# Retention in chunks of 64 tokens, two per visit, every product a 64x64 quarter of the array

## The chip, the cores and the metric

The kernel runs on one core of a Trainium2 chip. The metric is device time in microseconds (us), the median of several executions; for the kernel before it is 926.88 us over three runs (925.43 to 928.27). All times below that belong to an instruction come from one profiled execution.

## The reference: what is computed

Three layers follow one another on a batch of 8 sequences of 576 tokens. First comes retention with 8 heads of 64 channels, a causal product of queries, keys and values in which every pair of tokens is weighted with a power of the head's decay:

```
scores = q @ k.T / 8                       # per batch and head, 576 x 576
ret    = scores * gamma[h] ** (i - j)      # only where i >= j, else 0
x      = ret @ v                           # heads side by side: 576 x 512
```

Then a mixture of four single-head attentions (projections of x to 64 channels for q, k and v, causal softmax, output projection, the two best experts of four by a gate). Last a token and channel mixer (`x @ w_theta`, cosine and sine of it, two 576x576 token products, one 512x512 channel product).

Retention is not computed as 576 x 576 scores. The tokens are cut into chunks. Inside a chunk the masked scores are multiplied with the values; what lies before the chunk enters through a state, a 64x64 matrix per head, the running sum of `k.T @ v`, that is multiplied with the queries. The decays are put into the values and into a factor on the result, so that the mask is only 0 and 1.

## The kernel before

The first half of the program (to about 436 us) is one loop over 80 units: batch, expert pair, row block of attention (five row blocks of 128, 128, 128, 128 and 64 tokens). TensorE's order is the order in which the program is written (a manual schedule); the other engines' orders are laid down by a scheduler before the run. Ten units, numbered 0 to 9 here as *slots*, make one batch, and into the slots of batch b the retention of batch b+1 is woven. `SLOTS` says what each slot holds besides its attention: projections (`Q01`, `K10`, `v0` ...) and visits of the retention `R0` to `R5`. In this document an attention row block shows on TensorE as scores (`w<-KK,U`, line 309), transposes of the probabilities (`w<-ident,P`, line 356) and, in groups of row blocks, the outputs (`w<-PT,V`, line 375, function `at_out`), whose operand PT is copied out of the transposes' PSUM by VectorE (DVE) and ScalarE (ACT), line 361.

A visit Rc works on chunks of 128 tokens in four steps:

- `ret_values(c-1)`: the state's update (line 154, 128 rows by 64 columns of the array, two products side by side), the state's copy to SBUF by ACT (line 156), and scores times values (line 161, same half-width form)
- the attention outputs that are due
- `ret_state(c-1)`: state times queries (line 173, quarters of 64x64, 128 columns of data), then DVE multiplies the result with the decays into xt (line 181), ACT and GpSimd split xt into high and low parts
- `ret_scores(c)`: scores of the next chunk (line 132, quarters of 64x64, 128 or 64 columns), masked by DVE in six instructions per chunk (line 138 four times on 64 partitions, line 141 twice on 128)

All of these are fp32 products; each one shows as two records in the trace. The PSUM has eight banks: seven tiles `w` in a ring (`WB = 7`), through which all scores, transposes, projections, outputs and retention results go in the order of the program, and one bank `pS` for the state. A tile of the ring can be written again when the engine that reads it is done with the tile that had that place before, seven tiles earlier.

The chunks of batch 0 are done ahead of the loop, in the prologue. The last batch has a list of its own (`LAST`), with tiles of the mixer's first steps in place of retention; the second half of the program (480 us to the end) is the mixer.

Of the kernel before, what the change touches and what calls it, by code (L numbers as in the profile page):

```python
# [21 lines left out]
C = 128  # L22
# [5 lines left out]
NCONST = 256 + 192 + NCH * H + 1088 + E * E + 4 * (128 + NCH)  # L28
# [14 lines left out]
SLOTS = [("Q01 K10", "R0"), ("", ""), ("K11 Q10", ""), ("Q11", "R1"), ("", "R2"),  # L43
# [3 lines left out]
WB = 7  # L47
# [12 lines left out]
def tile_kernel(ctx: ExitStack, tc: tile.TileContext, qk, kv, w1, wo, wot, wd, cst, out):  # L60
# [21 lines left out]
    tri = att.tile([128, 3, 64], F32, name="tri")  # L82
    gam = att.tile([128, NCH, H], F32, name="gam")
# [8 lines left out]
    SB = [ret.tile([128, 4, D], F32, name=f"S{i}") for i in range(2)]  # L92

    SMT = [[ret.tile([128, 2, 2, 128], F32, name=f"sm{i}{q}") for q in range(2)] for i in range(2)]
# [14 lines left out]
    def loads(b, c):  # L109
        R = ROWS[c]  # L110
        o = c * 1024
        t = ret.tile([128, 8, R], F32, name="kt", bufs=LDB, padded_shape=[128, 8, 128])
        nc.sync.dma_start(t, qk[b, :, o:o + 8 * R].rearrange("p (h r) -> p h r", h=8))
        u = ret.tile([128, 2, DM], F32, name="kv", bufs=LDB)
        nc.sync.dma_start(u, kv[b, c * C:c * C + C, :].rearrange("r (a d) -> r a d", a=2))
        vp = ret.tile([128, H, D], F32, name="vp", bufs=VPB)
        MARK["pool"] = nc.gpsimd.tensor_mul(vp, u[:, 1, :].rearrange("p (h d) -> p h d", h=H),
                                            gam[:, c, :, None].to_broadcast([128, H, D]))
        QKT[b, c], KVT[b, c], VP[b, c] = t, u, vp

    def ret_scores(b, c):

        R = ROWS[c]
        t = QKT[b, c]
        ps = [ps1.tile([128, 2, 2, 128], F32, name="w", bufs=WB) for _ in range(2)]
        for i in range(2):
            for e, j in ((0, 0), (1, 0), (1, 1), (0, 1)):
                if j * 64 < R:
                    g = slice((e ^ j) * 64, (e ^ j) * 64 + 64)
                    for s in range(2):  # L130
                        r = slice(s * 64, s * 64 + 64)
                        nc.tensor.matmul(ps[s][g, i, e, j * 64:R], t[r, 4 + 2 * i + e, j * 64:j * 64 + 64],  # L132
                                         t[r, 2 * i + e, j * 64:R], start=True, stop=True, skip_group_check=True)
        sm = SMT[(b * NCH + c) % 2]
        for s in range(2):
            for e in range(2):
                g = slice(e * 64, e * 64 + 64)
                nc.vector.tensor_mul(sm[s][g, :, e, :64], ps[s][g, :, e, :64],  # L138
                                     tri[g, 2, None, :].to_broadcast([64, 2, 64]))
            if R > 64:  # L140
                nc.vector.tensor_mul(sm[s][:, :, :, 64:], ps[s][:, :, :, 64:],  # L141
                                     tri[:, None, 0:2, :].to_broadcast([128, 2, 2, 64]))
        SM[b, c] = sm

    def ret_values(b, c):
        R = ROWS[c]
        t, u, vp, sm = QKT.pop((b, c)), KVT.pop((b, c)), VP.pop((b, c)), SM.pop((b, c))
        if c == 0:
            PSS[b] = ps1.tile([128, 4, D], F32, name="pS", bufs=1, padded_shape=[128, 4, 128])
        if c < NCH - 1:  # L150
            pS = PSS[b]
            for h in range(H):
                s = h % 2 * 64
                nc.tensor.matmul(pS[s:s + 64, h // 2, :], u[:, 0, h * D:h * D + D], vp[:, h, :],
                                 start=c == 0 and h < 2, stop=False, skip_group_check=True)
            nc.scalar.activation(SB[(c + 1) % 2], pS, AF.Copy)
        px = [ps1.tile([128, 2, R], F32, name="w", bufs=WB, padded_shape=[128, 2, 256]) for _ in range(2)]
        for s in range(2):
            for i in range(2):
                for e in range(2):  # L160
                    nc.tensor.matmul(px[s][e * 64:e * 64 + 64, i, :], vp[:, 4 * i + 2 * e + s, :], sm[s][:, i, e, :R],
                                     start=i == 0, stop=not c and i == 1, skip_group_check=True)
        PX[b, c] = t, px

    def ret_state(b, c):
        R = ROWS[c]
        t, px = PX.pop((b, c))
        Sb = SB[c % 2]
        for i in range(2 if c else 0):
            for e in range(2):  # L170
                for s in range(2):
                    r, hp = slice(s * 64, s * 64 + 64), 2 * i + e
                    nc.tensor.matmul(px[s][e * 64:e * 64 + 64, i, :], Sb[r, hp, :], t[r, hp, :],
                                     start=False, stop=i == 1, skip_group_check=True)
# [5 lines left out]
        for s in range(2):  # L180
            nc.vector.tensor_mul(xt[:, 2 * s:2 * s + 2, :], px[s], gt[:, 2 * s:2 * s + 2, cs])
# [7 lines left out]
    def ret_out(b, c):  # L189
        ret_values(b, c)  # L190
        ret_state(b, c)

    def ret_first(b, names):
        for n in names.split():
            if n[0] == "R" and n != "R0" and b + 1 < B:
                ret_values(b + 1, int(n[1]) - 1)

    def ret_second(b, names):
        for n in names.split():
            if n[0] == "R" and b + 1 < B:  # L200
                c = int(n[1])
                if c:
                    ret_state(b + 1, c - 1)
                if c < NCH:
                    ret_scores(b + 1, c)
# [29 lines left out]
    def proj_v(b, c):  # L235
# [14 lines left out]
        nc.scalar.copy(V[:R, c, :, :], pv)  # L250
# [114 lines left out]
    def at_out(b, p, g):  # L365
# [13 lines left out]
        nc.scalar.copy(OB[b, p][:, ms[0] * C:ms[0] * C + W], po)  # L379
# [12 lines left out]
    o = 448  # L392
    nc.sync.dma_start(gam, cst[:, o:o + NCH * H].rearrange("p (c h) -> p c h", c=NCH))
    for s in range(2):
        for sm in SMT:
            for e in range(2):
                nc.gpsimd.memset(sm[s][64 - 64 * e:128 - 64 * e, :, e, :64], 0.0)
# [5 lines left out]
    nc.sync.dma_start(tri, cst[:, 256:448].rearrange("p (a q) -> p a q", a=3))  # L403
# [96 lines left out]
    ret_scores(0, 0)  # L500
    make_gt(0)
    ret_scores(0, 1)
    ret_out(0, 0)
    make_gt(1)
    for kt in range(4):
        split_w1(kt)
        if kt == 1:
            ret_out(0, 1)
# [3 lines left out]
    work(-1, "v0 v1")  # L512
    for c in range(2, NCH):
        ret_scores(0, c)
        ret_out(0, c)
        work(-1, ("", "v2 k00", "q00 v3 k01 v4 g")[c - 2])
# [13 lines left out]
    def token_tile(pp, g, i):  # L530
# [14 lines left out]
        if pp is ps1:  # L545
            if i % 2:
                th = pp.tile([128, DM], F32, name="w", bufs=WB)
            else:
                th = pp.tile([128, 4, 128], F32, name="pS", bufs=1).rearrange("p a d -> p (a d)")
# [51 lines left out]
    for t in range(nu + 1):  # L601
# [11 lines left out]
        if t == nu - 1:  # L613
# [3 lines left out]
            zp = pool("zp")  # L617
        if t:
# [4 lines left out]
        if b < B - 1:  # L623
            ret_first(b, between)
        else:
            work(b, between)
        if between or b == B - 1:
# [3 lines left out]
        if b < B - 1:  # L631
            ret_second(b, between)
# [249 lines left out]
```

## Time and profile before

| | |
|---|---|
| median of 3 runs | 926.88 us (925.43 to 928.27) |
| the profiled execution | 925.94 us, of which 924.2 us are the span of its instructions |
| TensorE (PE) matmuls busy | 887.6 us, 96% |
| VectorE (DVE) | 661.9 us, 72% |
| ScalarE (ACT) | 440.4 us, 48% |
| GpSimd (POOL) | 223.8 us, 24% |
| mean granted TensorE clock | 0.991 |

The busy time of PE is the time in which at least one matmul was under way, and matmuls overlap, so a busy PE may still stand behind a wait. What a run of matmuls costs is therefore read from the start of its first record to the start of the run that follows.

### The profile page before, as it was taken

To read this page: it belongs to the slowest core of one execution; us is meant where nothing else is said; L and a number is where in the kernel's file an instruction comes from. 1 tells how busy PE (TensorE), PEld (TensorE's weight loads), DVE (VectorE), ACT (ScalarE), POOL (GpSimd) and SP (SyncE) were. 2 spreads that over 40 slices of the span, in tenths; PEclk is the share of its full clock that TensorE was granted. 3 is DMA by queue.
4 is the path that set the end of the run, shared out by engine and by line. 5 is a ranking of instruction groups with operands and counts; after the bars stand their busy time and mean duration, and the time that the engine had idled before them with its cause. 6 is when DMAs were issued, how large, how long until landed. Compare 5 with 4: busy or idle time off the path is not lost.

```text
span 924.2 us, 22725 instructions
## 1 busy us (share of the span) xinstructions
PE 887.6 (96%) x8526; PEld 817.3 (88%) x8526; DVE 661.9 (72%) x2003; ACT 440.4 (48%) x1166; POOL 223.8 (24%) x276
## 2 busy tenths in 40 slices
PE   7899989999999999999999899999999999999998
PEld 6788978888888888888878899999999999999998
DVE  6487776877879787787777976766668674777632
ACT  2265645556556555555666533434334432444320
POOL 4316153361534525243121102102020110101010
PEclk8999999999999999999999899999999999999999
DMA  8667665776666776655685442343513333151311
GB/s 308 198 165 211 174 182 159 199 211 177 197 185 176 230 192 198 166 163 141 192 276 192 126 93 65 70 115 87 145 33 76 90 79 90 27 135 24 92 34 52
DMA packets 146205, 132.27 MB, mean 143 GB/s; under 512 B 83376, under 2 KB 121648, under 8 KB 146096
## 3 DMA queue, kind: packets, MB, share of 16 engines
q1 hardware_dynamic: 145952, 130.55, 50.5%
q8 instruction: 67, 1.10, 0.5%
q0 software_dynamic: 144, 0.28, 0.2%
q14 instruction: 42, 0.34, 0.1%
HBM read 80.20 MB, written 32.00 MB: 121 GB/s over the span
## 4 chain that ended last, share of the span: by engine, by line
PE 55%; DVE 7%; DMA 4%; ACT 3%; issue 2%; SPq 1%; POOL 1%; ACTq 0%; DVEq 0%; POOLq 0%
PE acc L712 22%; PE w L97 8%; PE w L99 8%; PE w L98 8%; PE w L375 3%; PE w L247 2%; PE w L309 2%; DMA KK<-KN 1%; ACT P L317 1%; DVE sm L138 1%; PE w L356 1%; DMA wost<-wot 1%; DMA og<-gd 1%; PE w L132 1%; DVE cs L577 1%
## 5 line engine op out<-in xcount | busy, mean ns | idle before, releaser
L712 PE MATMUL acc<-TK,zh 128*128 128x256 f32 (+1 forms) x1024 | 181.4, 300 | 3.9 <-DVE u L726 3.2
L712 PEld LDWEIGHTS acc<-TK,zh 128*128 128x128 f32 x1024 | 156.2, 192 | 4.5 <-ACT cs L575 3.4
L317 ACT ACTIVATE P<-P,st 128x128 f32<-128x128 f32 (+4 forms) x160 | 95.7, 600 | 68.0 <-DVE st L312 67.6
L712 PE MATMUL acc<-TK,zl 128*128 128x256 f32 (+1 forms) x512 | 110.7, 298 | 0.0
L728 POOL TENSOR_TENSOR ul<-u,uh 128x576 fp32r<-128x576 f32 x16 | 24.3, 1541 | 324.2 <-ACT uh L727 237.0
L712 PEld LDWEIGHTS acc<-TK,zl 128*128 128x128 f32 x512 | 87.4, 192 | 0.0
L102 ACT ACTIVATE zh<-cs 128x512 fp32r<-128x512 f32 x64 | 40.3, 631 | 90.1 <-PE acc L712 70.6
L375 PE MATMUL w<-PT,V 128*64 128x192 f32 (+3 forms) x576 | 67.1, 329 | 14.5 <-DVE PT L361 8.1
L97 PE MATMUL w<-xh,WH 128*128 128x288 f32 x256 | 76.6, 299 | 2.9 <-DVE sm L141 2.6
L103 DVE TENSOR_TENSOR zl<-cs,zh 128x512 fp32r<-128x512 f32 x64 | 44.9, 706 | 48.0 <-ACT zh L102 46.4
L309 PE MATMUL w<-KK,U 128*64 128x288 f32 (+4 forms) x384 | 77.8, 329 | 0.9 <-DMA KK<-KN 0.9
L575 ACT ACTIVATE cs<-cs 128x512 f32<-128x512 f32 x72 | 45.1, 631 | 67.4 <-DVE cs L573 54.0
L98 PE MATMUL w<-ul,CH 128*128 128x256 f32 (+1 forms) x256 | 75.7, 296 | 0.0
L375 PEld LDWEIGHTS w<-PT,V 128*64 128x64 f32 (+1 forms) x576 | 43.0, 138 | 36.9 <-ACT PT L361 13.2
L99 PE MATMUL w<-uh,CH 128*128 128x256 f32 (+1 forms) x256 | 75.7, 296 | 0.0
L97 PE MATMUL w<-uh,CH 128*128 128x256 f32 (+1 forms) x256 | 75.5, 297 | 0.1
L98 PE MATMUL w<-xl,WH 128*128 128x288 f32 x256 | 75.3, 294 | 0.0
L99 PE MATMUL w<-xh,WL 128*128 128x288 f32 x256 | 75.3, 294 | 0.0
L312 DVE CUSTOM_DVE_ANT_0 P<-w,cm 128x128 f32<-128x128 f32 (+4 forms) x160 | 72.2, 476 | 1.8 <-PE w L309 1.3
L138 DVE TENSOR_TENSOR sm<-w,tri 64x128 f32<-64x128 f32 x160 | 45.4, 284 | 25.5 <-PE w L132 17.7
L451 POOL TENSOR_TENSOR r<-r,ex 128x192 f32<-128x192 f32 (+1 forms) x51 | 29.5, 578 | 140.3 <-ACT P L317 52.0
L577 DVE SCALAR_TENSOR_TENSOR cs<-cs,x 128x512 f32<-128x512 f32 x72 | 48.8, 688 | 18.8 <-ACT cs L575 18.3
(142 smaller groups left out, 2192.5 us busy)
## 6 DMA issues: line engine op xcount, KB each, us to landing
kv<-kv SPq DMA_DIRECT2D x40, 512.0 KB
KK<-KN SPq DMA_DIRECT2D x128, 144.0 KB
kt<-qk SPq DMA_DIRECT2D x32, 512.0 KB
raw<-wd SPq DMA_DIRECT2D x43, 192.0 KB
xd<-xb SPq DMA_DIRECT2D x126, 64.0 KB
out<-u SPq DMA_DIRECT2D x28, 288.0 KB
u<-xd SPq DMA_DIRECT2D x28, 288.0 KB
td<-hl SPq DMA_DIRECT2D x27, 192.0 KB
```

Source lines behind the costliest of these rows:

```text
L97: nc.tensor.matmul(ps, ah, bh, start=first, stop=False)
L98: nc.tensor.matmul(ps, ah, bl, start=False, stop=False)
L99: nc.tensor.matmul(ps, al, bh, start=False, stop=last)
L103: nc.vector.tensor_sub(l, src, h)
L138: nc.vector.tensor_mul(sm[s][g, :, e, :64], ps[s][g, :, e, :64], tri[g, 2, None, :].to_broadcast([64, 2, 64]))
L309: nc.tensor.matmul(ps[s][:R], U[:, s, rs], KK[:, s, x, j0:j1], start=x == 0, stop=x == 1)
L312: MARK["dve"] = nc.vector.tensor_tensor_reduce(Ps[s][:R, j0:j1], ps[s][:R], cm[:R, o + j0:o + j1], 1.0, st[:R, 0, s:s + 1] if i else 3.0e3 ...
L317: MARK["act"] = nc.scalar.activation(Ps[s][:R, :n], Ps[s][:R, :n], AF.Exp, bias=st[:R, last, s:s + 1], scale=-1.0, accum_out=SUM[p][:R, m, ...
L375: nc.tensor.matmul(po[s * 64:s * 64 + 64, c0:], V[:ROWS[j], j, 2 * p + s, :], v, start=j == 0, stop=j == last, skip_group_check=True)
L575: nc.scalar.activation(cs, cs, AF.Sin)
L577: nc.vector.scalar_tensor_tensor(z, cs, -1.0, x2[:, None, ds].to_broadcast([128, 2, 256]), op0=OP.mult, op1=OP.mult)
L712: nc.tensor.matmul(acc[d][j], A[:, dc], TK[:, kt, W, t0:t1], start=q == 0 and n == 0, stop=q == 8 and n == 2)
```

## The change

Retention works on chunks of 64 tokens. A visit still handles two of them (128 tokens), but every product, scores, values, state and queries, is now 64 rows by 64 columns of the array with 64 columns of data, written in an order that goes round the four quarters. The operands are laid out on the host so that the halves of the partitions hold different heads.

The state of the first chunk of a visit is updated at the end of the visit before (`ret_state(2c)`), that of the second inside the visit (`ret_state(2c+1)`); four copies `S` in SBUF take turns. Products on different row halves of the array write to different PSUM banks, so the state has two banks and the ring is left with six (`WB = 6`). State times queries must write both banks from both row halves; it is cut into two parts, `ret_query(..., 0)` and `ret_query(..., 1)`, in which the row halves change banks, and the first product of the second part gets an explicit wait on an instruction of another engine that comes after the first part: the copy of the state by ACT, or in R5 the mask by DVE.

One attention output is issued inside each visit, between the next chunk's scores and the second query part. Outputs come later by one visit in part: that of slot 0 runs in slot 1 (`"O"`) before that slot's transposes, and of the two that fell into slot 3 one moves to slot 4. R0, the first scores of a batch, moves from slot 0 into R5 of the batch before. The mask is two DVE instructions per visit. State copies by ACT are eight per batch instead of four.

```diff
-SLOTS = [("Q01 K10", "R0"), ("", ""), ("K11 Q10", ""), ("Q11", "R1"), ("", "R2"),
+SLOTS = [("Q01 K10", ""), ("", "O"), ("K11 Q10", ""), ("Q11", "R1"), ("", "R2"),
          ("v0", "R3"), ("v1", ""), ("v2 k00", "R4"), ("q00", "R5"), ("v3 k01 v4 g", "")]
-WB = 7
+WB = 6
...
     def ret_scores(b, c):
+        for j in range(n):
+            for i in range(2):
+                for v in range(2):
                     for s in range(2):
+                        x = 2 * v + i
+                        nc.tensor.matmul(ps[s][half(v), j, i, :], t[half(s), 4 + x, half(j)], t[half(s), x, half(j)],
+                                         start=True, stop=True, skip_group_check=True)
...
+            MARK["sync"] = nc.vector.tensor_mul(sm[s][:, :n], ps[s][:, :n], tri[:, None, None, :].to_broadcast([128, n, 2, 64]))
...
+    def ret_state(b, k):
+        c, j = divmod(k, 2)
...
+            PSS[b] = ps1.tile([128, 2, 512], F32, name="pS", bufs=1)
...
+        MARK["sync"] = nc.scalar.activation(SB[(k + 1) % 4], pS[:, :, :2 * D].rearrange("p v (i d) -> p v i d", i=2), AF.Copy)
...
+    def ret_query(b, c, cross, sync=None):
...
+                for s in range(2):
+                    v = s ^ cross
+                    mm = nc.tensor.matmul(px[v][half(i), s, j, :], SB[k % 4][half(s), v, i, :],
+                                          t[half(s), 2 * v + i, half(j)], start=False, stop=False, skip_group_check=True)
+                    if sync:
+                        tc.add_manual_dep(mm.ins, sync.ins.name, SYNC, reason="the row halves change banks")
+                        sync = None
...
+    def ret_step(b, c, nx, other):
+        if c >= 0:
+            ret_values(b, c)
+            ret_query(b, c, 0)
+            MARK["sync"] = None
+            if c < NCH - 1:
+                ret_state(b, 2 * c + 1)
+            done = MARK["sync"]
+        if nx:
+            ret_scores(*nx)
+        other()
+        if c >= 0:
+            ret_query(b, c, 1, done or MARK["sync"] or MARK["out"])
+            ret_end(b, c)
+        if nx and nx[1] < NCH - 1:
+            ret_state(nx[0], 2 * nx[1])
...
+    ret_step(0, 2, (0, 3), lambda: work(-1, "v0"))
+    ret_step(0, 3, (0, 4), lambda: work(-1, "v1"))
+    ret_step(0, 4, None, lambda: work(-1, "v2 k00"))
+    ret_step(1, -1, (1, 0), lambda: None)
+    work(-1, "q00 v3 k01 v4 g")
...
+        if between == "O":
+            for o in outs:
+                at_out(*o)
+            outs = []
         if t:
             at_trans(units[t - 1])
...
+            if between[:1] == "R":
+                def other():
+                    at_out(*outs.pop(0))
+                c = int(between[1])
+                x = b + 1
+                ret_step(x, c - 1, (x, c) if c < NCH else (x + 1, 0) if x + 1 < B else None, other)
```

On TensorE, slot 4 of a batch (visit R2) before, from the last transposes to the next unit's scores; the shapes are partitions by columns of the result:

```order
L356 MATMUL w<-ident,P 128x128 x8
L154 MATMUL pS<-vp,kv 64x64 x8
L161 MATMUL w<-sm_135,vp 64x128 x4
L161 MATMUL w<-sm_136,vp 64x128 x4
L173 MATMUL w<-kt,S_134 64x128 x8
L132 MATMUL w<-kt 64x128 x4
L132 MATMUL w<-kt 64x64 x4
L132 MATMUL w<-kt 64x128 x4
L132 MATMUL w<-kt 64x64 x4
L309 MATMUL w<-KK,U 128x128 x4
```

The same slot now, from the second half of the values on (line 166 is line 161 of before, 179 is 173, 153 is 154, 135 is 132, 391 is 375, 325 is 309):

```order
L166 MATMUL w<-sm_137,vp 64x64 x4
L166 MATMUL w<-sm_138,vp 64x64 x4
L179 MATMUL w<-kt,S_135 64x64 x4
L179 MATMUL w<-kt,S_136 64x64 x4
L153 MATMUL pS<-vp,kv 64x64 x8
L135 MATMUL w<-kt 64x64 x16
L391 MATMUL w<-PT,V 64x256 x4
L391 MATMUL w<-PT,V 64x128 x2
L179 MATMUL w<-kt,S_135 64x64 x4
L179 MATMUL w<-kt,S_136 64x64 x4
L153 MATMUL pS<-vp,kv 64x64 x8
L325 MATMUL w<-KK,U 128x128 x4
```

An attention output of half-width form (line 391) has come in between scores and the second query part, and the state stands twice, once ahead of the scores and once at the end.

On ACT, the same slot before, from the output of slot 3 to the split of xt (S is the state's copy, P the exponentials of the unit's row block, PT the copy that the attention outputs read, r and hl weight conversions):

```order
L379 COPY ob<-w 128x256
L156 ACTIVATE S_133<-pS 128x256
L317 ACTIVATE P,sum_126<-P,st 64x576 x2
L361 COPY PT<-w 128x4x128
L450 ACTIVATE r<-raw 128x192
L183 ACTIVATE xh<-xt 128x4x128
```

And now (line 333 is 317, 377 is 361, 462 is 450, 464 is 452, 155 is 156, 395 is 379, 199 is 183):

```order
L333 ACTIVATE P,sum_126<-P,st 64x576 x2
L377 COPY PT<-w 128x4x128
L462 ACTIVATE r<-raw 128x192
L464 ACTIVATE hl<-b_4439 128x192
L155 ACTIVATE S_133<-pS 128x256
L395 COPY ob<-w 128x256
L155 ACTIVATE S_134<-pS 128x256
L199 ACTIVATE xh<-xt 128x4x128
```

The state's copy, which stood ahead of the two exponentials, has moved behind them, behind the PT copy and behind two conversions; the second query part on TensorE waits for the first of the two copies.

## Rows read from the trace of the kernel before

**Rows 1.** Windows: us, busy PE, PEld, DVE, ACT, POOL; granted clock, DMA share, GB/s

```profile
0.00:44.38 44.38, 35.08 (x498) 30.75 (x499) 24.61 (x52) 12.13 (x26) 18.08 (x32) 0.92 0.80 259
212.32:268.47 56.15, 54.31 (x692) 48.32 (x690) 45.07 (x169) 33.25 (x106) 23.16 (x31) 1.00 0.68 193
```

**Rows 2.** Lines by form, PE, retention: line, rows*columns of array, form, records | busy, mean

```profile
L161 PE MATMUL w<-sm,vp 128*64 128x128 f32 x512 | 34.2, 274 | 2.4 <-DVE sm L141 2.4
L132 PE MATMUL w<-kt 64*64 64x128 f32 x512 | 25.4, 277 | 1.4 <-DMA kt<-qk 1.4
L132 PE MATMUL w<-kt 64*64 64x64 f32 x640 | 23.8, 217 | 0.0
L154 PE MATMUL pS<-vp,kv 128*64 128x64 f32 x512 | 21.9, 228 | 0.0
L173 PE MATMUL w<-kt,S 64*64 64x128 f32 x384 | 16.6, 280 | 0.0
L161 PE MATMUL w<-sm,vp 128*64 128x64 f32 x128 | 6.2, 230 | 0.8 <-DVE sm L138 0.8
L173 PE MATMUL w<-kt,S 64*64 64x64 f32 x128 | 3.7, 230 | 0.0
```

**Rows 3.** Timeline, PE, visit R2 (slot 4): start us, us, line, form, records

```profile
235.28 0.69 PE L154 MATMUL pS<-vp,kv 128*64 128x64 f32 x16
235.79 1.05 PE L161 MATMUL w<-sm,vp 128*64 128x128 f32 x16
236.77 0.67 PE L173 MATMUL w<-kt,S 64*64 64x128 f32 x16
237.26 0.85 PE L132 MATMUL w<-kt 64*64 64x128 f32 x32
238.03 0.44 PE L309 MATMUL w<-KK,U 128*128 128x128 f32 x2
```

**Rows 4.** Timeline, PE, visit R5 (slot 8), last chunk of 64 tokens

```profile
258.66 0.69 PE L161 MATMUL w<-sm,vp 128*64 128x64 f32 x16
259.18 0.61 PE L375 MATMUL w<-PT,V 128*64 128x256 f32 x2
260.51 1.30 PE L375 MATMUL w<-PT,V 128*64 128x256 f32 x10 [0.73 <-ACT PT L361]
261.74 0.46 PE L173 MATMUL w<-kt,S 64*64 64x64 f32 x16
262.13 0.61 PE L309 MATMUL w<-KK,U 128*64 128x288 f32 x3
```

**Rows 5.** Waits to 440 us: who waited for whom: us in total, times, longest

```profile
PEld w L173 <- issue: 4.1, 24, 0.2
PE w L375 <- DVE PT L361: 7.3, 12, 3.0
PE w L375 <- ACT PT L361: 5.7, 11, 0.7
```

**Rows 6.** Lines by form to 440 us, masks on DVE, state copies on ACT

```profile
L138 DVE TENSOR_TENSOR sm<-w,tri 64x128 f32<-64x128 f32 x160 | 45.4, 284 | 25.5 <-PE w L132 17.7 <-DMA tri<-cst 6.4
L141 DVE TENSOR_TENSOR sm<-w,tri 128x256 f32<-128x256 f32 x64 | 27.2, 425 | 0.9
L156 ACT ACTIVATE S<-pS 128x256 f32<-128x256 f32 x32 | 12.4, 387 | 28.2 <-PE pS L154 28.2
```

**Rows 7.** Timelines of slots 3 and 4: transposes (PE), U and xt (DVE), PT (ACT)

```profile
228.21 0.82 PE L356 MATMUL w<-ident,P 128*128 128x128 f32 x6
...
230.34 0.93 DVE L233 SCALAR_TENSOR_TENSOR U<-w,U 64x288 fp32r<-64x288 f32 x2
...
238.10 0.56 ACT L361 COPY PT<-w 128x512 f32<-128x512 f32 x1
```

**Rows 8.** Timeline, PE, prologue, chunk 2 of batch 0

```profile
24.43 0.69 PE L154 MATMUL pS<-vp,kv 128*64 128x64 f32 x16
25.77 0.66 PE L161 MATMUL w<-sm,vp 128*64 128x128 f32 x8 [0.65 <-DVE sm L141]
```

More of the change, by code (lines that the diff above doesn't have):

```diff
@@ L113, in loads @@
         nc.sync.dma_start(t, qk[b, :, o:o + 8 * R].rearrange("p (h r) -> p h r", h=8))
[L114 to L118, printed above, removed]
+        n = R // 64
@@ L121, in ret_scores @@
     def ret_scores(b, c):
-        R = ROWS[c]
+        n = ROWS[c] // 64
         t = QKT[b, c]
[L125 to L129, printed above, removed]
+        ps = [ps1.tile([128, 2, 2, 64], F32, name="w", bufs=WB, padded_shape=[128, 4, 2, 64]) for _ in range(2)]
+        for j in range(n):
+            for i in range(2):
+                for v in range(2):
@@ L143, in ret_scores @@
-        SM[b, c] = sm
-    def ret_values(b, c):
-        R = ROWS[c]
[L147 to L163, printed above, removed]
@@ new lines, in ret_scores @@
+        SM[b, c] = sm
+    def ret_state(b, k):
+        c, j = divmod(k, 2)
+        u, vp = KVT[b, c], VP[b, c]
+        if k == 0:
+            PSS[b] = ps1.tile([128, 2, 512], F32, name="pS", bufs=1)
+        pS = PSS[b]
+        for i in range(2):
+            for s in range(2):
+                for v in range(2):
+                    x = 2 * s + i
+                    nc.tensor.matmul(pS[half(s), v, i * D:i * D + D], u[half(v), j, 0, x * D:x * D + D], vp[half(v), j, x, :],
+                                     start=k == 0 and i == 0, stop=False, skip_group_check=True)
+        MARK["sync"] = nc.scalar.activation(SB[(k + 1) % 4], pS[:, :, :2 * D].rearrange("p v (i d) -> p v i d", i=2), AF.Copy)
@@ new lines, in ret_values @@
+    def ret_values(b, c):
+        n = ROWS[c] // 64
+        vp, sm = VP[b, c], SM.pop((b, c))
+        px = [ps1.tile([128, 2, 2, 64], F32, name="w", bufs=WB, padded_shape=[128, 4, 2, 64]) for _ in range(2)]
+        PX[b, c] = px
+        for j in range(n):
+            for s in range(2):
+                for i in range(2):
+                    for v in range(2):
+                        nc.tensor.matmul(px[v][half(i), s, j, :], vp[half(v), j, 2 * s + i, :], sm[s][half(v), j, i, :],
+                                         start=j == 0 and s == 0, stop=False, skip_group_check=True)
@@ L175, in ret_state, with ret_end @@
+    def ret_end(b, c):
+        R = ROWS[c]
+        px = PX.pop((b, c))
+        for x in (QKT, KVT, VP):
+            x.pop((b, c))
         cs = slice(c * C, c * C + R)
@@ L249, in proj_v @@
         pv = ps[:R, :E * D].rearrange("p (e d) -> p e d", e=E)
-        nc.scalar.copy(V[:R, c, :, :], pv)
+        MARK["out"] = nc.scalar.copy(V[:R, c, :, :], pv)
         nc.scalar.activation(l[:R, c, :], ps[:R, E * D:], AF.Copy)
@@ L391, in tile_kernel @@
         nc.tensor.matmul(pw, warm, warm, start=True, stop=True)
[L392 to L397, printed above, removed]
+    o = 320
+    nc.sync.dma_start(gam, cst[:, o:o + NCH * H].rearrange("p (c j h) -> p c j h", c=NCH, j=2))
     for l in LG:
```

115 lines of the change are left out of this document (41 added, 74 removed).

## Prediction

> **What bounds the kernel now.** I read the windows of the profile first: busy time of each engine, batch by batch. In a typical batch TensorE (PE) is busy for 54.3 of 56.2 us, DVE for 45.1, ACT for 33.3 [rows 1]; the loop over the 80 units is bound by PE, with DVE second. Seven batches carry visits, and the prologue (44.4 us, PE busy 35.1) carries the retention of batch 0 [rows 1]. The second half of the program does not change.
>
> The groups by line and form come next: how many records of each kind retention has [rows 2]. Their mean durations are no price, since matmuls overlap. The price is read from the timeline of one visit, from the start of a run to the start of the next [rows 3, 4]. Then the waits [rows 5]: where PE stands, it stands before an attention output, for the copy PT. All runs are at the same clock level, so the prices carry over.
>
> **Prices from rows.**
> - State, half-width, 64 columns: 16 records from 235.28 to 235.79, 32 ns each [rows 3].
> - Values, half-width, 128 columns: 16 from 235.79 to 236.77; about 0.1 us of it belongs to the change of form that follows, so 55 ns each [rows 3]. With 64 columns (16 from 258.66 to 259.18) 32 ns [rows 4].
> - Quarters, 128 columns: 16 from 236.77 to 237.26, less 0.05 us for the change ahead: 27.5 ns [rows 3].
> - Quarters, 64 columns: 16 from 261.74 to 262.13, 0.39 us, of which one whole change of form (0.17, below) is taken off: 14 ns [rows 4]. The mixed run of 32 scores confirms it: 16 x 27.5 + 16 x 14 = 0.66, and 0.77 is seen with the change behind it [rows 3].
> - A change of the array's form: PE idles 4.1 us in 24 cases ahead of line 173, with nothing waited for that the profile shows: 0.17 us each [rows 5].
>
> **The change part by part.**
>
> *Products.* Before: 512 x 55 + 128 x 32 (values), 512 x 32 (state), 384 x 27.5 + 128 x 14 (queries), 512 x 27.5 + 640 x 14 ns (scores): 28.2 + 4.1 + 16.4 + 10.6 + 1.8 + 14.1 + 9.0 = 84.2 us, counts from [rows 2]. Now a batch has nine chunks of 64: 72 products for scores, 72 for values, 64 for state, 64 for queries, 272 in all, two records each; in eight batches 4352 records of the 64-column quarter kind, at 14 ns 60.9 us. The sum falls by 23.3 us. The number of records rises by half, so this term hangs on the 14 ns. They are seen in runs of 16 records; the new runs are about 100 long. From the other side the price is bounded by the 27.5 ns of the wider quarters: then the term is 119.7 - 84.2 = 35.5 us of loss. I take the 14 ns, because those rows have exactly the new form.
>
> *Changes of form.* Before, each of six visits goes full, half, quarter, full: 18 per batch. Now the five visits that are left go full, quarter, half (the output), quarter, full, and slot 1's output alone makes two: 22. Four more in seven batches at 0.17 us cost 4.8 us. The Trainium skill, "TensorEngine Tiling (Array Packing)", section Key Properties, says that changing the tiling mode drains TensorE. The trace agrees with 0.17 us a time, and this is the one rule that speaks against writing an output into the middle of a visit; it costs a fifth of what the products give.
>
> *Waits that go.* PE idles 13.0 us in 23 cases before outputs for PT [rows 5]. The idle time counts from the modelled end of the record before; in R5 the start stands 1.33 us behind a pair of records that fills 0.22, so 1.1 us are lost where 0.73 are noted [rows 4]. With 0.35 more each, the waits are 13.0 + 23 x 0.35 = 21 us, 3 per batch. In the new order the outputs in slots 1, 3 and 4 belong to an earlier slot, and their PT has long been copied; the others have a visit's products ahead of them as before. I take all 21 out and count what remains as new waits.
>
> *New waits.* Four places, per batch.
>  - Slot 3: the ring of six. The second tile of the next scores takes the bank that the projection `Q11` had. DVE is done with that at 230.34 + 0.93 = 231.27, 2.3 us after the transposes' run ended at 228.96 (start of the state's run there) [rows 7]. PE reaches the scores after a change 0.17, values 0.45, queries 0.11, state 0.22: 0.95. It waits 1.3. With seven banks and two outputs ahead of the scores it did not.
>  - Slot 4: the second query part waits for the state's copy, which on ACT has moved behind two exponentials, PT and two conversions. PT ends at 238.66 [rows 7], then three instructions of about 0.39, the copy's own mean [rows 6] (an estimate for the other two): 239.83, 4.55 us after the transposes' run (235.28). PE needs it after 0.17 + 0.45 + 0.22 + 0.22 + 0.45 + 0.17 and an output of about 1.3 + 0.17 (ten records took 1.23 with their change [rows 4]): 3.15. That would be 1.4 of wait. But the exponentials hang on DVE, and a visit's masks fall from 4 x 0.284 + 2 x 0.425 = 1.99 to 0.85 us [rows 6]: 1.14 earlier. I take 0.5, between 0.3 and 1.4. Queued behind the waiting product on PE are the rest of the visit and the next scores; DVE's xt and with it two banks of the ring wait for them.
>  - Slot 5: the first tiles after that visit take the banks of its two results, free only when xt is done, which DVE does after masks and conversions: 1.0, between 0.4 and 2.0.
>  - Slot 8: the output still waits for PT; products ahead of it take 1.1 instead of 0.5 us: 0.5 left of 1.1.
>  Together 3.3 per batch, 23 us in seven; from 1.3 (only slot 3) to 6.0 per batch, 9 to 42 us.
>
> *DVE and ACT.* Masks are 64 x 0.425 + 16 x 0.284 = 31.7 us instead of 72.6 [rows 6]: 41 us less on the second engine. ACT gains 32 copies at 0.387, 12.4 us [rows 6], beside 12 us per batch in which it has nothing to do at PE's pace. Neither is added: the loop goes by PE, and what they move is in the waits above.
>
> *Prologue.* The values of chunks 2 to 4 stand between state and mask, as at 24.43 + 0.51 to 25.77, 0.83 us [rows 8], and again ahead of their second half. Now scores run a visit ahead, with projections in between; but two of these start later, and R0 is added. I take 3 us, between 6 gained and 1 lost, beyond the prologue's share of the products. The last batch goes on with six banks where seven were; nothing to 2 us, not in the sum.
>
> **Sum:** -23.3 + 4.8 - 21 + 23 - 3 = -19.5 us. The profiled execution took 925.94, close to the median of 926.88; off the median that is 907 us.
>
> **Rivals.**
> 1. *The waits eat it.* The ring of six and the copy's place cost the upper end, 6.0 per batch (42 instead of 23), and the last batch's 2: 907 + 19 + 2 = 928. For it: DVE and ACT work in a fixed order and lag by 2 to 4.5 us in slots 3 to 5 [rows 7]. Against it: the masks' 1.14 us per visit fall in just these slots.
> 2. *The other side: long runs of quarters don't keep 14 ns.* Place: the block of about 100 records in each visit. Price: at 21 ns, midway to the wider quarters' rate, 4352 x 7 ns = 30 us, so 938; at 27.5 ns 59 us, so 966. It decides from 14 + 19.5 / 4.352 = 18.5 ns. For it: PE must be handed a record and its weights every 14 ns for 1.4 us on end; before, only short stretches ask for that, and the 48 records from 236.77 to 238.03 average 26 ns [rows 3]. Against: in that same stretch the 64-column records behind the wide ones still fit 14. The Trainium skill, "TensorE: Matmul & The Clock Gate", section Wait - 56ns, not 53.3ns?, says that the distance from start to start never falls below about 25 ns, however few the columns; by that the products would cost 109 us instead of 61. The rows disagree where four quarters take turns: 0.39 us for 16, even with the change counted in, is 24 ns, and 14 without.
> 3. *DVE's relief pays more.* If shorter masks let PT, the state's copy and the banks come in time everywhere but slot 3, the new waits are 9 us: 907 - 14 = 893.
>
> **How the numbers follow.** The forecast 907 has 0.60, its own range 896 to 920; the waits (928) 0.16, the slow quarters (938 and above) 0.11, the relief (893) 0.13. The range of 889 to 928 leaves out most of the slow quarters, half of the first rival's upper side and the far end of the third. Within 0.3% is 924.1 to 929.7, about what three runs of this kernel can tell from no change. Faster than that: 0.58 of the forecast's 0.60, 0.05 of the first rival, all of the third: 0.76. Within: 0.02 + 0.06 = 0.08. Slower: 0.11 + 0.05 = 0.16.
>
> **What the profile after will show.** 64-column quarter records at 14 ns from start to start in a visit, about 1.4 us from values to scores without a wait (right), or 20 and more (rival 2). PE waits of lines 391 and 179 and of the ring in slots 3 to 5: about 3 us a batch (right), 6 (rival 1), 1 (rival 3). A batch of 56 us should take about 54, the prologue about 39. DVE's busy time should fall by 41 us and ACT's rise by 12 in the first half. The forecast is wrong if a batch still takes 56, or if the waits at outputs have not moved.

## The result, and the profile after

The changed kernel takes **910.2 us** (median of 4 runs, 910.16 to 912.79) against 926.8 us (925.43 to 928.27) beside it: ratio 0.982, 95% interval 0.980 to 0.984, so 16.6 us faster by the medians. The forecast was 907. The profiled execution of the changed kernel took 912.79 us, the longest of the four, so the two traces show 13.2 of the 16.6 us.

From the start of one slot's attention scores to the next, the trace says where: the prologue takes 41.0 us instead of 44.4, the seven batches with visits 382.2 instead of 391.9, the rest of the program the same (484.1 and 484.6, to the end of the last matmul). But by the same measure a batch of the changed kernel holds more waits than was thought. The windows of prologue and one batch after (columns as in [rows 1]):

```profile
0.00:41.02 41.02, 31.94 (x738) 29.52 (x739) 17.67 (x36) 13.90 (x31) 16.01 (x24) 0.88 0.82 273
207.25:262.08 54.83, 51.56 (x884) 46.30 (x882) 45.63 (x151) 34.86 (x110) 22.98 (x31) 1.00 0.67 193
```

A batch is 1.3 us shorter than the one in [rows 1], and PE is busy for 2.7 us less of it: half of what PE no longer does has become idle time. DVE is no less busy in this batch than in the one before, although its masks are lighter (the last section says what took their place).

The lines by form after, retention on PE, masks and state copies (to be held against [rows 2] and [rows 6]):

```profile
L179 PE MATMUL w<-kt,S 64*64 64x64 f32 x1024 | 32.8, 229 | 6.5 <-ACT S L155 5.6 <-ACT ob L395 0.5
L135 PE MATMUL w<-kt 64*64 64x64 f32 x1152 | 29.0, 226 | 6.3 <-ACT lg L267 2.6 <-DVE PT L379 2.0 <-DMA kt<-qk 1.3
L153 PE MATMUL pS<-vp,kv 64*64 64x64 f32 x1024 | 27.5, 222 | 3.7 <-POOL vp L118 3.7
L166 PE MATMUL w<-sm,vp 64*64 64x64 f32 x1152 | 26.8, 229 | 3.0 <-DVE sm L139 3.0
...
L139 DVE TENSOR_TENSOR sm<-w,tri 128x256 f32<-128x256 f32 x64 | 23.8, 413 | 14.1 <-PE w L135 8.1 <-DMA tri<-cst 5.7
L139 DVE TENSOR_TENSOR sm<-w,tri 128x128 f32<-128x128 f32 x16 | 3.9, 285 | 6.5 <-PE w L135 6.5
...
L155 ACT ACTIVATE S<-pS 128x256 f32<-128x256 f32 x64 | 24.4, 382 | 25.9 <-PE pS L153 25.9
```

The 4352 records are there, idle time stands before all four groups, masks cost 27.7 us instead of 72.6, state copies 24.4 instead of 12.4. Visit R2 of the changed kernel, the counterpart of [rows 3], with ACT's side of it below:

```profile
226.85 0.70 PE L166 MATMUL w<-sm,vp 64*64 64x64 f32 x32
227.37 0.41 PE L179 MATMUL w<-kt,S 64*64 64x64 f32 x16
227.60 0.41 PE L153 MATMUL pS<-vp,kv 64*64 64x64 f32 x16
227.83 0.65 PE L135 MATMUL w<-kt 64*64 64x64 f32 x32
228.41 1.30 PE L391 MATMUL w<-PT,V 128*64 128x256 f32 x12
230.64 0.46 PE L179 MATMUL w<-kt,S 64*64 64x64 f32 x16 [0.93 <-ACT S L155]
230.92 0.41 PE L153 MATMUL pS<-vp,kv 64*64 64x64 f32 x16
231.26 0.91 PE L325 MATMUL w<-KK,U 128*128 128x128 f32 x3
```

```profile
228.50 0.56 ACT L377 COPY PT<-w 128x512 f32<-128x512 f32 x1
228.97 0.38 ACT L462 ACTIVATE r<-raw 128x192 f32<-128x192 uint32 x1
229.95 0.36 ACT L464 ACTIVATE hl<-b 128x192 fp32r<-128x192 f32 x1 [0.60 <-DVE b L459]
230.22 0.36 ACT L155 ACTIVATE S<-pS 128x256 f32<-128x256 f32 x1
```

From 226.85 to 227.83 stand 64 quarter records in 0.98 us, 15 ns each with one step of 87 ns behind the fourth, where 39 are usual, counted in. Then the second query part waits for the state's copy, which stands on ACT behind PT and two conversions, the second of which waits for DVE itself. In slot 8 (R5), which answers to [rows 4], the wait has changed sides, from the output to the ring:

```profile
251.65 0.28 PE L135 MATMUL w<-kt 64*64 64x64 f32 x2
252.43 0.69 PE L135 MATMUL w<-kt 64*64 64x64 f32 x30 [0.51 <-DVE PT L379]
253.05 1.30 PE L391 MATMUL w<-PT,V 128*64 128x256 f32 x12
```

The waits of PE from 40 to 430 us, after ([rows 5] has those of before; L377 and L379 are the copies PT, L263 the projection of the values, L98 the others):

```profile
PE w L179 <- ACT S L155: 5.6, 10, 1.6
PE w L263 <- POOL xl L200: 4.2, 2, 2.7
PE w L135 <- ACT lg L267: 2.6, 5, 0.7
PE w L98 <- POOL xl L200: 2.5, 5, 1.0
PE w L391 <- ACT PT L379: 2.4, 7, 0.4
PE w L325 <- DVE sm L139: 2.2, 4, 1.0
PE w L135 <- DVE PT L379: 2.0, 4, 0.5
```

The view's rows sum to 15.6 us before and 23.1 after. The outputs hardly wait any more (13.0 to 2.7), and much around them does.

The two waits of line 263 for xl, the longest of all (2.7 us), have another cause than the copies. Both times xl stands on GpSimd right behind `vp<-kv,gam` (line 118, the values of a later chunk times the decays), and GpSimd sits idle until the load of kv is there, a DMA transfer: 7.11 us until 73.57 and 2.77 us until 130.65. xl starts 1.0 and 1.2 us after vp.

### The profile page after: what moved, and what is told of

Its sections match the earlier page's. It is cut to its first block, busy times and chain, and to the rows that moved or that the text cites. A ratio compares the mean times of both kernels' runs of the same rounds, so it can differ in the third digit from the quotient of the medians.

```text
span 910.9 us, 25606 instructions
## 1 busy us (share of the span) xinstructions
PE 866.0 (95%) x10062; PEld 800.9 (88%) x10062; DVE 645.3 (71%) x1859; ACT 454.4 (50%) x1198; POOL 220.2 (24%) x268
## 4 chain that ended last, share of the span: by engine, by line
PE 66%; DVE 14%; DMA 8%; ACT 5%; issue 3%; POOL 2%; SPq 1%; ACTq 0%; POOLq 0%; DVEq 0%
PE acc L730 22%; PE w L98 9%; PE w L97 9%; PE w L99 9%; PE w L263 4%; PE w L325 3%; DMA kv<-kv 3%; PE w L391 3%; PE w L372 2%; ACT P L333 2%; DVE P L328 2%; DMA KK<-KN 2%; DVE U L249 1%; DVE xt L196 1%; DVE sm L139 1%
## 5 line engine op out<-in xcount | busy, mean ns | idle before, releaser
L103 DVE TENSOR_TENSOR zl<-cs,zh 128x512 fp32r<-128x512 f32 x64 | 47.5, 745 | 48.0 <-ACT zh L102 47.5
L98 PE MATMUL w<-xl,WH 128*128 128x288 f32 x256 | 76.2, 298 | 2.5 <-POOL xl L200 2.5
L98 PE MATMUL w<-ul,CH 128*128 128x256 f32 (+1 forms) x256 | 75.7, 296 | 0.0
L325 PEld LDWEIGHTS w<-KK,U 128*128 128x128 f32 (+1 forms) x384 | 54.4, 171 | 10.2 <-DVE sm L139 3.5
L391 PE MATMUL w<-PT,V 128*64 128x192 f32 (+3 forms) x576 | 56.9, 325 | 3.8 <-ACT PT L379 2.4
L372 PE MATMUL w<-ident,P 128*128 128x128 f32 (+2 forms) x480 | 59.5, 259 | 0.7 <-DVE ML L103 0.4
L118 POOL TENSOR_TENSOR vp<-kv,gam 128x512 f32<-128x512 f32 (+1 forms) x40 | 39.4, 985 | 79.1 <-DMA kv<-kv 52.7
```

The costliest lines, as they stand in the source:

```text
L98: nc.tensor.matmul(ps, ah, bl, start=False, stop=False)
L103: nc.vector.tensor_sub(l, src, h)
L325: nc.tensor.matmul(ps[s][:R], U[:, s, rs], KK[:, s, x, j0:j1], start=x == 0, stop=x == 1)
L372: nc.tensor.transpose(tp[:w, j, :], Ps[s][:R, j * C:j * C + w], ident[:R, :R])
L391: nc.tensor.matmul(po[s * 64:s * 64 + 64, c0:], V[:ROWS[j], j, 2 * p + s, :], v, start=j == 0, stop=j == last, skip_group_check=True)
```

## The experiments

All were timed beside the kernel before (medians 926.3 to 927.5); the changed kernel is 910.2. Each ratio is to the kernel before.

**Single parts of the change, made in the kernel before**

*Outputs moved only.*

```
-SLOTS = [("Q01 K10", "R0"), ("", ""), ...
+SLOTS = [("Q01 K10", "R0"), ("", "O"), ...
...
+        if between == "O":
+            for o in outs:
+                at_out(*o)
+            outs = []
...
+        elif between[:1] == "R" and between != "R0":
+            at_out(*outs.pop(0))
```

> The kernel before with one part of the change alone: the attention outputs in the new places (slot 0's in slot 1 ahead of that slot's transposes, one output per visit), products and ring as before. By my account of the change the waits of slots 0 and 3, about 1 us per batch, go, and one change of form per batch comes (0.17): 7 - 1 = 6 us less, about 921. Rival: the places of the outputs are most of the whole gain; then 12 us or more less, 915 or below. Second rival: they only pay together with the shorter visits; then 925 to 928.

Measured 915.8 us, ratio 0.989 (0.987 to 0.991): 10.7 us faster. The places of the outputs are worth this without any quarter product.

*Ring of six only.*

```
-WB = 7
+WB = 6
```

> The kernel before with a ring of six banks instead of seven and nothing else. If the ring is what the changed kernel pays with (the waits ahead of its scores in slots 3, 5 and 8, some 2 us per batch), the old order pays as well, since there too the banks of six tiles earlier come free only just in time in slots 4 and 5: 8 to 15 us more, 935 to 942. Rival: the seventh bank was hardly used, within 2 us of 926.8.

Measured 938.1 us, ratio 1.012 (1.010 to 1.014): 11.6 us slower. Where it waits:

```profile
PE w L375 <- DVE PT L361: 10.8, 12, 2.6
PE w L375 <- ACT PT L361: 7.0, 10, 0.8
```

A part of the bank's price shows at the outputs, where PE already waited in [rows 5] (7.3 and 5.7): 4.8 us more. Another 4.7 us stand ahead of attention scores (line 309), which had no row of their own in this view before.

*Light masks only.* The 64-partition masks of a full chunk go, and with them part of the scores.

```
-            for e in range(2):
+            for e in range(1 if R == 64 else 0):
                 g = slice(e * 64, e * 64 + 64)
                 nc.vector.tensor_mul(sm[s][g, :, e, :64], ps[s][g, :, e, :64], ...
...
+                nc.gpsimd.memset(sm[s][64 * e:64 + 64 * e, :, e, :64], 0.0)
```

> The kernel before with 144 of its 160 masks on 64 partitions left out (all four of each full chunk, two of four in each last chunk), so that the scores of each full chunk's first 64 queries enter as zeros; TensorE's products and their order are those of before. DVE has 41 us less (144 x 284 ns), as after the change. Theory that the lighter DVE is worth about half of its time wherever it stands (45 us more cost 24 us in the changed kernel): 903 to 912 us. Rival, the forecast's own term (the loop goes by TensorE, DVE's relief is not added): 921 to 927 us. Between the two: with seven banks DVE has more slack than with six, so 912 to 921 us would say that the worth depends on the ring.

Measured **909.9 us**, ratio 0.981 (0.979 to 0.983): 17.6 us faster, at the upper end of the first theory and far from the rival. With TensorE's program unchanged, 41 us less of masks (DVE's whole busy time falls by 32, 661.9 to 629.7) give as much as the whole change. The waits of PE, 40 to 430 us:

```profile
PE w L375 <- DVE PT L361: 6.9, 12, 1.2
PE w L375 <- ACT PT L361: 2.8, 3, 0.9
```

By the measure of the table below, seven batches take 380.2 us instead of 391.9, and the difference lies at the outputs (51.7 instead of 58.4) and the attention scores (55.7 instead of 60.9); the other kinds are as before.

*All three.* Edits of the three above together, with the same part of the scores left out.

> The kernel before with the outputs in the changed kernel's manner (one in each visit, slot 0's in slot 1), a ring of six banks and the same 144 masks left out (the same part of the scores enters as zeros): all that the change does beside the form of its products, the query product in two parts and the state in two banks. If the single steps add up (-10.7, +11.6, and -20 for the masks): about 907 us, and the quarter products with their mode changes, waits and moved state copies are then worth nothing net. If the forecast's net for the products holds (-23.3 of products, +4.8 of mode changes, up to +10 of new waits against the changed kernel's 910.2): 920 to 930 us.

Measured 906.5 us, ratio 0.977 (0.974 to 0.979), below the changed kernel's ratio, and the intervals do not overlap. The single steps sum to -10.7 + 11.6 - 17.6 = -16.7; together they give -21. So the form of the products, with the split queries, the state in two banks and the eight copies that it brings, is worth nothing net: 4 us lost by the medians, 5 by the ratios. Two smaller parts of the change are in this remainder too, since this kernel keeps R0 in slot 0 and has the output ahead of the queries, not behind the next scores; the expectation's "all that the change does beside" passes over them. The waits of PE in this kernel, 40 to 430 us, and its visit R2:

```profile
PE w L375 <- DVE PT L361: 1.9, 4, 0.7
PE w L247 <- POOL xl L184: 1.1, 2, 0.8
```

```profile
222.21 0.69 PE L154 MATMUL pS<-vp,kv 128*64 128x64 f32 x16
222.72 1.04 PE L161 MATMUL w<-sm,vp 128*64 128x128 f32 x16
223.60 1.25 PE L375 MATMUL w<-PT,V 128*64 128x256 f32 x12
224.78 0.67 PE L173 MATMUL w<-kt,S 64*64 64x128 f32 x16
225.27 0.85 PE L132 MATMUL w<-kt 64*64 64x128 f32 x32
226.04 0.66 PE L309 MATMUL w<-KK,U 128*128 128x128 f32 x4
```

With the old, slower products the visit runs from 222.21 to 226.04, 3.83 us, without a gap; the changed one needs 226.85 to 231.26, 4.41 us. The view's waits are 4.3 us here and 23.1 in the changed kernel: the difference, 19 us, is about what the products were to save (23.3 - 4.8 = 18.5).

The two side by side, seven batches, each record from its start to the start of the next, summed by kind (us):

| | values | state | queries | scores | outputs | projections | attention scores | all |
|---|---|---|---|---|---|---|---|---|
| old products, three edits | 31.4 | 14.4 | 12.6 | 27.1 | 46.3 | 142.6 | 56.9 | 372.6 |
| changed kernel | 16.7 | 16.1 | 16.3 | 30.0 | 50.6 | 150.5 | 60.7 | 382.2 |

(Transposes, 41 in both, are in the sum.) Only the values gain. The scores have about three quarters of their old price in work (1152 records at 14.6 ns are 16.8 us, where the forecast has 23.1 for the old ones) and come out dearer; the ring's wait stands inside their run (4.6 us in the view's rows for line 135). The table overstates the loss: these two executions took 904.95 and 912.79 us, 7.8 apart, where the medians are 3.7 apart. A little of it is TensorE's clock, granted at the lower level (1.2 GHz) for 3.5 us of the changed kernel's batches, from 134.4 to 137.9, behind its longest wait for xl, and nowhere in the batches of the other.

**The change taken back or loaded in part**

*Outputs in the old places.*

```
-SLOTS = [("Q01 K10", ""), ("", "O"), ...
+SLOTS = [("Q01 K10", "O"), ("", ""), ...
... (the block of "O" moves behind the transposes)
-                    at_out(*outs.pop(0))
+                    while outs:
+                        at_out(*outs.pop(0))
```

> The changed kernel, with the attention outputs back in the places of before (slot 0's in slot 0 behind its transposes, both of slot 3 in R1, none in R2), still between the next scores and the second query part. If the outputs' places give what they gave in the kernel before (10.7 us): 921. More, if R2 without an output leaves the state's copy uncovered (1.3 us per batch, 9 in all): 925 to 930. Rival: the waits at outputs only trade places with the waits of the ring: 910 to 914.

Measured 942.6 us, ratio 1.017 (1.014 to 1.019): 32 us slower than the changed kernel.

```profile
PE w L263 <- POOL xl L200: 17.8, 6, 3.5
PE w L179 <- ACT S L155: 10.6, 7, 2.5
```

In the new order the outputs' places are worth three times as much as in the old one, and most of the waiting comes in slot 7, at the values' projection. There xl is not late for want of xt: in the batch from 157 us on, xt is done at 191.01 and its high part xh at 191.67. GpSimd has vp next, and vp waits for the load of kv, issued at 191.18:

```profile
195.51 1.04 POOL L118 TENSOR_TENSOR vp<-kv,gam 128x512 f32<-128x512 f32 x1 [4.94 <-DMA kv<-kv]
196.51 1.26 POOL L200 TENSOR_TENSOR xl<-xt,xh 128x512 fp32r<-128x512 f32 x1
```

All six waits of line 263 have such a vp ahead of xl, for whose load GpSimd sat idle for 4.1 to 4.9 us. A part of the 32 us is TensorE's clock. Five stretches in the batches, 20.6 us together, ran at the lower of its two levels (granted 0.50 to 0.51), where the changed kernel has one of 3.5; each begins during a wait of PE of 2.3 to 3.5 us or within 1.2 us of its end. Records of lines 97 to 99 stand 0.24 us apart there and 0.13 at full clock, so the 17 us more cost at most some 8 (an estimate from these steps).

*Masks made heavier.* Four masks of 64 partitions added per visit.

```
+            for v in range(2):
+                g = half(v)
+                nc.vector.tensor_mul(sm[s][g, 0], ps[s][g, 0], tri[g, None, :]...)
```

> The changed kernel, with four more masks on 64 partitions per visit ahead of the two that are needed (their results are written over), as many DVE instructions as the kernel before had: 45 us more on DVE. If the loop goes by PE and DVE's relief buys little, as the forecast has it: 0 to 4 us more, 910 to 914. If the relief is what keeps xt and the banks of the ring in time: a visit's 1.1 us fall on the path in three to five of five visits per batch, 20 to 35 us more, 930 to 945.

Measured 934.0 us, ratio 1.009 (1.006 to 1.012): 24 us slower, as the theory of a tight DVE had it. But (line 182 is 179, 142 is 139):

```profile
PE w L182 <- DVE sm L142: 12.1, 6, 2.7
```

An amount like half of it stands at one place, slot 8, where the second query part has the explicit wait on a mask. That part needs the new wait and the heavier mask together; the worth of the lighter masks is therefore taken from the kernel before (17.6). Another 7.8 us stand ahead of the attention scores of slot 5, for nothing that the profile shows.

*Scores made twice.*

```
-        for j in range(n):
+        for j in [j for j in range(n) for _ in range(2)]:
```

> The changed kernel, with every product of the retention's scores done twice (the second overwrites the first; same result): 1152 more records of the 64-column quarter kind. If their price is the 14.6 ns that the trace shows in whole visits and all of it is on the path: 16.8 us more, 927. If long runs cost more than short ones, or 27 ns each as wide quarters do: 31 us, 941. Rival: the visits wait anyway (ring, copy of the state), so that a third or more of the products' time is hidden: 918 to 922.

Measured 922.9 us, ratio 0.995 (0.993 to 0.997): 12.7 us slower for 1152 more records, 16.8 us at 14.6 ns. PE's time still counts, at three quarters; the rest disappears in waits (17.7 us in the view instead of 23.1).

**Attempts on the new waits**

*The state's copy first on ACT.* Conversions must come behind it.

```
-        MARK["sync"] = nc.scalar.activation(SB[(k + 1) % 4], ...
+        MARK["act"] = MARK["sync"] = nc.scalar.activation(SB[(k + 1) % 4], ...
```

> The changed kernel, with weight conversions put behind the copy of the state on ACT, so that the copy on which the second query part waits runs two conversions (0.74 us) earlier in slots 3 and 4. The trace after shows 0.3 us of this wait per batch in slot 3 and 0.57 in slot 4, 6 us in seven batches. If it is a cost of its own: 3 to 5 us less, 905 to 907. Rival: behind it stands another wait (the exponentials ahead of the copy, xt, the ring), and nothing is gained: 909 to 911.

Measured 918.7 us, ratio 0.992 (0.989 to 0.994): 8.5 us slower than the changed kernel.

```profile
PE w L391 <- DVE PT L379: 7.2, 4, 2.7
PE w L325 <- DVE sm L139: 6.5, 8, 1.2
PE w L98 <- POOL xl L200: 4.7, 3, 3.3
```

The wait for the copy goes from this list, and what comes is larger. That the later conversions make DVE and the ring late fits these rows but is not shown by them; the longest wait for xl, 3.3 us, stands again behind a vp for whose load GpSimd sat idle for 7.7 us.

*Output ahead of the scores in R1, R2 and R4.*

```
+        early = b and c in (0, 1, 3)
+        if early:
+            other()
         if nx:
             ret_scores(*nx)
-        other()
+        if not early:
+            other()
```

> The changed kernel, with the output ahead of the next chunk's scores in visits R1, R2 and R4, where its operand belongs to an earlier slot; R3 and R5 as they are. The scores' second tile then has 0.4 to 1.3 us more before it needs its bank of the ring. If the ring is a cost of its own: the 0.47 us ahead of slot 3's scores go, 3 us less, 907. Rival: the second query part needs the state's copy at the same time as before, and the wait only moves there: 909 to 911.

Measured 911.9 us, ratio 0.984 (0.982 to 0.986): no difference.

*Projections in other slots, to change the ring's order.*

```
-... ("K11 Q10", ""), ("Q11", "R1"), ("", "R2"), ("v0", "R3"), ("v1", ""), ("v2 k00", "R4"), ("q00", "R5"), ("v3 k01 v4 g", "")]
+... ("K11 Q10 Q11", ""), ("", "R1"), ("", "R2"), ("", "R3"), ("v0 v1", ""), ("v2 k00", "R4"), ("v3", "R5"), ("q00 k01 v4 g", "")]
```

> The changed kernel, with four projections in other slots and nothing else: Q11 from slot 3 to slot 2, v0 from 5 to 6, q00 and v3 exchanged between 8 and 9. In slots 3, 5 and 8 the second tile of the next scores needs the bank of a projection (Q11, v0, q00) that stands six tiles earlier; now that bank belongs to attention scores or to v3, which are read sooner. If the ring's order is the cause of the waits ahead of those scores (0.47, 0.65 and 0.6 us per batch in the trace after): 12 us less in seven batches, some 5 of it lost to other waits, 898 to 905. Rival: the lateness of DVE and ACT is the cause, whichever tile comes six earlier, and the waits move to the next tile: 908 to 912.

Measured 910.7 us, ratio 0.984 (0.981 to 0.986): no difference.

*Conversions without the guard*, and *the same with the moved projections*.

```
-        nc.vector.tensor_scalar(ex, hi, 0x7FF00000, None, op0=OP.bitwise_and)
-        nc.vector.scalar_tensor_tensor(v, ex, float(0x38100000), v, op0=OP.is_ge, op1=OP.mult)
```

> The changed kernel with two of the five DVE instructions of each weight conversion left out (the guard that sets values below the smallest normal number to zero), some 37 us less on DVE in the loop. If DVE is the second bound that half of the loop's waits go back to: 891 to 900 us. Rival, that what DVE has left is hidden behind TensorE: 906 to 910 us.

> As the one before (conversions without the guard), with three pieces of projection moved to other slots (the second half of Q11 to slot 2, v0 to slot 6, q00 and v3 exchanged between slots 8 and 9). The same move was worth nothing in the changed kernel. If the waits that remain come from the ring's order once DVE is lighter: 3 to 6 us below the kernel without the move. If they come from late copies alone: within 2 us of it.

Measured 912.3 us, ratio 0.983 (0.981 to 0.985), and 912.9 us, ratio 0.984 (0.982 to 0.986): no difference in either. DVE's busy time fell by 20 us in the first (645.3 to 624.9), and nothing came of it. The expectation's 37 was too high, since a neighbour took over part of the time: the 43 instructions of line 455, an untouched step, rose from 16.1 to 23.1 us. The waits of PE in the first:

```profile
PE w L263 <- POOL xl L200: 8.8, 4, 3.0
PE w L179 <- ACT S L155: 2.9, 6, 1.3
```

Against the changed kernel the copy S gains 2.7 us and xl loses 4.6. The four waits of line 263 stand behind a vp for whose load of kv GpSimd sat idle for 2.4 to 6.8 us, so what took the gain's place here is a transfer and GpSimd's order, not DVE. At two of them (from 75.9 and from 188.5) TensorE ran at the lower clock level for 3.4 us; the changed kernel has one such stretch in its batches. So DVE's time has no price of its own: 32 us less of it in the kernel before, by lighter masks, came with 17.6 us, 20 us less in the changed one, by lighter conversions, with nothing. Whether lighter conversions would pay with the load in time, or whether DVE has slack by now, or whether conversions count for less since they hold no ring tile as masks do, no run here tells: none lightens the conversions of the kernel before or moves the load.

No kernel here that computes all of the reference beats the changed one.

## Why the time was right and its reasons only in part

The time came out 3 us above the forecast, inside its own range. The sum had the right size by terms that do not hold one by one, and that they cancel is luck: 18.5 us were credited to the products, which bring nothing net, and nothing to the lighter masks, which alone bring 17.6.

- **Price of the products: right.** 14 ns were forecast, 15 are seen over 64 records in a visit, 14.6 over 80 (1165 ns). 4352 records are 63.5 us instead of 60.9. The slow quarters of the second rival are out.
- **Changes of form, 4.8: about right, by a row that was misread.** The 4.1 us of [rows 5] are waits of the weight loads (PEld), not idle time of PE. In visit R2 of the changed kernel a change into quarters costs 0.14 us (201 ns from the last transpose to the first quarter record, where transposes are 108 apart, and 87 instead of 39 behind the fourth), one out of them 0.11 (148 instead of 39). The trace has 32 more changes of all kinds in seven batches, where 28 were forecast.
- **What the products are worth: wrong.** -23.3 + 4.8 stood in the sum as time off the path. The kernel with the other three edits and the old products is as fast or faster, so their 18.5 us were not gained. The changed kernel has 19 us more of waits in the view: for the copy S, for the ring inside the scores, for xl. That these waits are what took the gain is read from the two traces; no run keeps the new products and removes the waits.
- **Lighter DVE, "Neither is added: the loop goes by PE": this is the step that failed.** The masks alone give 17.6 us, nearly the forecast's whole sum. The masks' saving was counted about right (41 forecast, 44.9 seen), their price of nothing was not. DVE's whole busy time fell by 16.6 us only (661.9 to 645.3), where 41 were promised. [rows 1] had DVE busy for 45.1 of 56.2 us, and the outputs' waits in [rows 5] were for copies that DVE and ACT make; the forecast gave the relief only to the second query part in slot 4. (ACT's "12 us per batch in which it has nothing to do" does not follow from [rows 1], which leave it 22.9 idle; the sum does not use it.)
- **Output waits, -21: half.** Moved outputs alone give 10.7.
- **New waits, +23 in four places: right in size, one place missing.** In the changed kernel, start to start less the price, each batch holds 0.8 us in slot 3, 0.6 in slot 4, 1.1 in slot 5 and 0.7 in slot 8 on average: 3.2 where 3.3 were forecast. Not foreseen is xl: 0.5 in slot 9, and up to 2.9 in slot 7 of the first two batches; with it 4.4 per batch, as many as before (4.2). In slot 7 the cause is the load of kv ahead of xl on GpSimd, which no term and no rival has. Waits of this size were the first rival's mechanism, which came in part. The ring's price alone is +11.6 in the old order, at other places.
- **Prologue, -3 beside the products: 3.4 in all.** The forecast had 3 more from the products. The light masks alone bring it from 44.4 to 41.8, the three edits together only to 43.6; the runs don't settle whose the 3.4 are.
- **The last batch with six banks**: nothing, as taken (484.1 against 484.6).

What was promised for the profile held in part: 54.6 us for a batch instead of 54, the prologue 41 instead of 39, masks 45 us less, ACT's copies 12 more. "The waits at outputs have moved" was to confirm the forecast, and it came with a larger sum of waits; as a sign it could not tell the products' gain from DVE's.

The third rival, that DVE's relief pays more, was right about DVE and wrong about the time: the waits of the new form took the relief's extra gain.

## What to carry to other kernels

An engine at 70 to 80% busy beside a bound engine at 96% need not be free. Here masks, which sit between PSUM tiles and their reuse, paid in the old program, and conversions, which don't, paid nothing in the new one. Take such an engine's share of a change out alone, on the old program, before crediting the new product form. Work saved on the bound engine is a gain only as far as the copies that it needs arrive earlier by the same amount; here 18.5 us of faster products came with 19 us more of waits. Where an order is fixed ahead of the run, removing the largest wait (the state's copy) can cost more than it returns. And a wait for one engine's result can be a wait for a transfer: look at what stands ahead of the result on that engine, here a product that waits for its load.

## What the runs showed of the hardware that was not expected

Quarters of 64 columns that go round the four parts of the array keep 14 to 15 ns from start to start as long as nothing waits: 92 records in 1.30 us in a visit of the changed kernel, 124 in 1.77 us where the scores are made twice. They start in rounds of four, one for each part: three steps of 5 to 8 ns and one of 38 to 40.

DVE and GpSimd stand in each other's way. A weight conversion is five DVE instructions on tiles that lie in SBUF. The lines by form for one of them, 43 times the same work, first in the kernel before, then in the changed one:

```profile
L445 DVE TENSOR_SCALAR ex<-raw 128x192 int32<-128x192 int32 x43 | 12.2, 284 | 1.9 <-POOL r L451 1.9
```

```profile
L457 DVE TENSOR_SCALAR ex<-raw 128x192 int32<-128x192 int32 x43 | 20.6, 479 | 0.0
```

And two rows of the changed kernel's timeline, DVE and GpSimd:

```profile
241.30 1.35 DVE L457 TENSOR_SCALAR ex<-raw 128x192 int32<-128x192 int32 x1
...
241.22 1.31 POOL L200 TENSOR_TENSOR xl<-xt,xh 128x512 fp32r<-128x512 f32 x1
```

The instruction ends 0.12 us after GpSimd's does. Of the 51 executions of line 457 (the smaller conversions too) 14 start while a GpSimd instruction is under way; they last 519 to 1379 ns, 1007 on average. The other 37 last 254 ns at most, among them seven in which a GpSimd instruction starts later. The five lines together (the 128x192 form) take 89.3 us instead of 74.3, as much as a third of the 45 us that the masks gave up. The Trainium skill, "SBUF — State Buffer", section "SBUF: two separate sides", says that the two engines share a pair of ports as an exclusive lock, which goes to whichever instruction starts first and is held for all of it; on DVE's side it names instructions in a two-port mode or with two inputs in SBUF. These rows agree with it; that the lock is the cause, and that line 457 runs in such a mode, no run here singles out.
